# Attention and two MoE layers on one core: later head pairs in key chunks of 128, with the last 64 keys of two pairs packed on four quarters of the array

## The chip, the core and the metric

One core of a Trainium2 chip runs the whole program. The metric is the time on the device in microseconds (us). TensorE (PE) multiplies matrices and writes PSUM, VectorE (DVE), ScalarE (ACT) and GpSimd (POOL) work elementwise, SyncE (SP) issues most DMAs. The kernel before takes 728.23 us, the median of 3 runs (727.34 to 729.0).

## What is computed

Attention over 4 batches, 12 heads, 448 positions, head size 64, then an MLP with a softmax gate and a layer norm, then a mixture of 8 experts. Only the first part is touched:

```python
scores = scale * np.matmul(q, k.transpose(0, 1, 3, 2))
scores = cap * np.tanh(scores / cap)
scores = scores - np.max(scores, axis=-1, keepdims=True)
attn = np.exp(scores)
attn = attn / (np.sum(attn, axis=-1, keepdims=True) + 1e-09)
return np.matmul(attn, v).astype(np.float32)
```

The kernel leaves the row maximum out (the cap bounds the exponent) and divides by the sums at the end.

## The kernel before, in words

Two heads make a pair; pair (b, p) is batch b and heads 2p and 2p+1, and its number is n = 6b + p, 0 to 23. Scores are held transposed, keys on the partitions and 448 queries along the row, so that one tile holds both heads (896 columns). The 448 keys of a pair are cut into four chunks of 112 (`CK`).

A **unit** (`unit`, L949) handles half a pair: `cp` 0 makes the scores of chunks 0 and 1, `cp` 1 those of chunks 2 and 3. Within a unit the order is: scores (`a_scp`, L739), Tanh and Exp on ACT (L765, L770), the product with V (`a_av`, L788), and filler. In a unit with `cp` 1 the V product is that of chunks 0 and 1 of the same pair; in a unit with `cp` 0 it is that of chunks 2 and 3 of the pair before. So V always lags one unit behind the scores.

The first 8 pairs (`PLAIN`) multiply raw float32. From pair 8 on keys and queries are split into a high and a low part of a faster type (kh, kl, qh, ql; `a_split`, L722), and each chunk takes three products, each of two matmuls on the two 64-row halves of the array, one for each head (L758). The V product is plain float32: two matmuls on the two 64-column halves (L800), and in the profile each float32 matmul is two instructions. The sums over keys are first added up on DVE into `es` (`a_esp`, L773: three additions of 896 columns for a pair, L780, L783, L784) and then multiplied with a column of ones on 32-column strips, four at a time, once for two pairs (L812).

**PSUM.** Pool `psA` (L442) has three tiles of two banks under one tag: scores, the MLP's h and y, its transposes lt, and the small tiles sum, rt and rb all take turns in them. Pool `psS` has one bank for the V product (tag B, `btile`, L481) and one for the sums (S). So the V product of a pair cannot start before the copy of the pair before into X has freed the bank (L819, on DVE, or on ACT for some pairs).

**The filler.** From pair 8 on the MLP of the batch before runs in small steps between the attention blocks: `m_h`, `m_act`, `m_tr`, `m_y`, put in by `fill` (L918) at a rate, and by `settle` (L925) when a model of the clock holds that no psA tile is free. `a_fin2` (L855) multiplies a finished batch by its reciprocal sums: three tiles rb_0, rb_1, rb_2, which `finish` (L930) puts into the units of pair p = 1.

**Order.** From pair 8 on only PE's order is written by hand (L1036); ACT, DVE, POOL and SP are ordered ahead of time by a scheduler. Every engine runs its own list strictly in order.

Of the kernel before, what the change touches and what calls it, by code (L numbers as in the profile page):

```python
# [10 lines left out]
F32 = mybir.dt.float32  # L11
F32R = mybir.dt.float32r
F16 = mybir.dt.float16
I32 = mybir.dt.int32
# [8 lines left out]
P = 128  # L23
CK = 112
# [59 lines left out]


@with_exitstack
def attn_moe_kernel(ctx, tc, kq, vv, w_in, w_out, packed, ids, mbias, w1, w2, out):
    nc = tc.nc
    pe, act, dve, pool, sp = nc.tensor, nc.scalar, nc.vector, nc.gpsimd, nc.sync

# [15 lines left out]
    wg_t = pk[:, 1 + NF:]  # L106
    sc8 = con.tile([P, 1], F32, name="sc8")
    epsv = con.tile([P, 1], F32, name="epsv")
    zone = con.tile([CK, 63], F32, name="zone")
    comb = con.tile([P, H], F32, name="comb")  # L110
    sel = con.tile([P, NP, P], F32R, name="sel")
    rh = con.tile([P, S], F32R, name="rh")
# [364 lines left out]
    def atile(nm):  # L477
        clock.take(nm)
        return psA.tile([P, 2, 512], F32, tag="A", name=nm)
# [217 lines left out]
    def direct(b, p):  # L697
        return b * NP + p < DIRECT

    def plain(b, p):  # L700
        return b * NP + p < PLAIN
# [13 lines left out]
            raws[b, p] = [t[:, 0, :], t[:, 1, :]]  # L715

    def v_load(b, p):
        v = ap_.tile([CK, 4, P], F32, tag="v", name=f"v{b}_{p}")
        (act if b * NP + p < VACT else sp).dma_start(out=v, in_=vv[b, p])
        vt[b, p] = v  # L720

    def a_split(b, p, which):  # L722
# [9 lines left out]
    et, est = {}, {}  # L732

    def e_new(nm):
        return ap_.tile([CK, 2, S], F32, tag="e", name=nm, bufs=5)

    exps = {}

    def a_scp(b, p, cp):  # L739

        chunks = (2 * cp, 2 * cp + 1)
        ps = []
        if plain(b, p):
            products = [raws[b, p]]
        else:
            (kh, kl), (qh, ql) = spl[b, p]
            products = [(kh, qh), (kh, ql), (kl, qh)]
        if not plain(b, p):
            settle(2)
        for c in chunks:  # L750
            if not plain(b, p):
                settle()
            t = atile(f"sc{b}_{p}_{c}")
            ps.append(t)
            for i, (k, q) in enumerate(products):
                for j in range(2):
                    r = slice(64 * j, 64 * j + 64)
                    pe.matmul(t[:CK, j, :S], k[r, c * CK:c * CK + CK], q[r], start=(i == 0), stop=(i == len(products) - 1))  # L758
            clock.spend(0.62, "rows")
            clock.work(1.05)  # L760
            clock.leave(f"sc{b}_{p}_{c}", clock.act - clock.t + 0.1)
        clock.work(2.1)
        es = [e_new(f"e{b}_{p}_{c}") for c in chunks]
        for e, t in zip(es, ps):
            act.activation(e, t[:CK, :, :S], AF.Tanh, scale=sc8[:CK])  # L765
        exps[b, p, cp] = es

    def a_exp(b, p, cp):
        for c, e in zip((2 * cp, 2 * cp + 1), exps.pop((b, p, cp))):
            act.activation(e, e, AF.Exp, scale=cap_t[:CK])  # L770
            et[b, p, c] = e

    def a_esp(b, p, cp):  # L773

        if direct(b, p):
            return
        e = [et[b, p, c] for c in (2 * cp, 2 * cp + 1)]
        if cp == 0:
            s = est[b, p] = ap_.tile([CK, 2, S], F32, tag="est", name=f"es{b}_{p}", bufs=2)
            dve.tensor_add(s, e[0], e[1])  # L780
        else:
            s = est[b, p]
            dve.tensor_add(s, s, e[0])  # L783
            dve.tensor_add(s, s, e[1])  # L784

    avt, spt = {}, {}

    def a_av(b, p, chunks=range(4)):  # L788

        if 0 in chunks:  # L790
            avt[b, p] = btile(f"av{b}_{p}")
            if p == 0:
                spt[b] = psS.tile([P, 512], F32, tag="S", name=f"S{b}")
        o, v = avt[b, p], vt[b, p]
        clock.spend(0.75 * len(chunks), "columns")
        if direct(b, p) or p % 2 and 3 in chunks:
            clock.spend(0.75, "strips")
        for c in chunks:
            for j in range(2):
                pe.matmul(o[64 * j:64 * j + 64, :S], v[:, c, 64 * j:64 * j + 64], et[b, p, c][:, j, :],  # L800
                          start=(c == 0), stop=(c == 3))
        if direct(b, p):
            for c in chunks:
                for j in range(2):
                    g = 2 * j + c % 2
                    pe.matmul(spt[b][32 * g:32 * g + 32, :S], zone[:, 31 - p:63 - p], et[b, p, c][:, j, :],  # L806
                              start=(p == 0 and c < 2), stop=(p == NP - 1 and c > 1))
        elif p % 2 and 3 in chunks:
            for j in range(2):
                for i in range(2):  # L810
                    g, pp = 2 * j + i, p - 1 + i
                    pe.matmul(spt[b][32 * g:32 * g + 32, :S], zone[:, 31 - pp:63 - pp], est[b, pp][:, j, :],  # L812
                              start=(p == 1), stop=(p == NP - 1))
        if 3 in chunks:
            x = xtile(b)[:, p, :]
            if convs and b + p:
                later["x"].append(lambda: dve.tensor_copy(x, o[:, :S]))
            else:
                (dve.tensor_copy if b * NP + p in XCD else act.copy)(x, o[:, :S])  # L819
            if p == NP - 1:  # L820
                a_ssb(b)

    sums = {}

    def a_ssb(b):
        ssb = ap_.tile([P, S], F32, tag="es", name=f"ssb{b}", bufs=2)
        act.copy(ssb, spt[b][:, :S])
        sums[b] = ssb
# [120 lines left out]
    def unit(n, cp):  # L949
        nonlocal mp  # L950
        b, p = pairs[n]
        early = plain(b, p) and b > 0
        strips, trs = later["strip"], later["pe"]
        later["strip"], later["pe"] = [], []

        def run(fs):
            while fs:
                fs.pop(0)()

        a_scp(b, p, cp)  # L960
        if n == 1 and not cp:
            a_av(*pairs[0], chunks=(2, 3))
        flush("cast")
        if early and p:
            flush("gate")
            if not cp:
                finish(b - 1, 4)
            else:
                run(strips)
                flush("gate")  # L970
                cv.release()
                mp = tc.alloc_tile_pool(name="mp", bufs=2, reuse_waits="tile")
                do_step()
        a_exp(b, p, cp)
        if early and cp and not p:
            flush("gate", "sub")
            finish(b - 1, 2)
        if cp == 0 and n > 1:
            a_av(*pairs[n - 1], chunks=(2, 3))
        elif cp:  # L980
            a_av(b, p, chunks=(0, 1))
        if convs:
            convs.pop(0)()
        flush("gate", "x")
        run(strips)
        flush("gate")
        if early and p and not cp:
            finish(b - 1, 5)
        run(trs)
        if early and cp and not p:  # L990
            flush("gate")
            finish(b - 1, 3)
        fill(FW[0])
        if b > 0 and not plain(b, p):
            finish(b - 1, 4 * p + 2 * cp)
        flush("sub")
        if n == 1 and cp:
            setup_third(*tables)
        a_esp(b, p, cp)
        if n + 1 < len(pairs):  # L1000
            a_split(*pairs[n + 1], cp)
        fill(FW[1])
        if cp == 1 and n + 2 < len(pairs):
            a_load(*pairs[n + 2])
        if cp == 0 and n + 1 < len(pairs):
            v_load(*pairs[n + 1])
        fill(FW[2])
        if b > 0 and not plain(b, p):
            finish(b - 1, 4 * p + 2 * cp + 1)
        while early and p and sums_:  # L1010
            conv_og(sums_[0], atile(f"po{sums_.pop()}")[:, 0, :NE])
# [24 lines left out]
    with tc.manual_schedule(engines={ET.PE}):  # L1036
        for n in range(FIXED, len(pairs)):
            unit(n, 0)
            unit(n, 1)
        a_av(B - 1, NP - 1, chunks=(2, 3))  # L1040
        for _ in range(ENDS[0]):
            do_step()
        a_sums(B - 1)
        for _ in range(ENDS[1]):
            do_step()
        a_recip(B - 1)
        t = (B - 1) * S // P - 1
# [683 lines left out]
```

## Time and profile before

| | |
|---|---|
| median of 3 runs | 728.23 us |
| the profiled execution: its own time | 729.04 us |
| its span, first to last instruction | 727.2 us |
| TensorE clock granted, of full speed | 0.998 |
| PE / weight loads / DVE / ACT busy | 99% / 76% / 60% / 53% |
| pairs 8 to 23 | about 93 to 366 us of the span |

The span is the core's time line; the profiled execution's own time is 1.84 us longer. A busy share counts the time in which at least one instruction of the engine runs. In the chain of waits, a row gives a start, a length and the work that set the end there; a block such as "sc x12" is a run of 12 matmul instructions.

### The profile page before, as it was taken

The page shows a single profiled execution, that of the slowest core. Times are in us where ns is not written, and L with a number is a line of the kernel's source. Part 1 is how long each engine was busy: PE and PEld are TensorE (multiplying, and loading weights), DVE is VectorE, ACT ScalarE, POOL GpSimd, SP SyncE. Part 2 cuts the span into 40 slices and gives each one's busy share as a digit, 9 for nine tenths or more (in the row PEclk, how much of TensorE's full clock was granted, in tenths as well). Part 3 has the DMA queues.
Part 4 walks back from the last instruction along what each step waited for, and adds up shares of the span by engine and source line. Part 5 has one row for each costly group of instructions (what it writes and reads, how often), then busy time and mean ns, then how long its engine had stood idle before and what let it go on. Part 6 is the DMA issues. An engine that isn't in the chain of part 4 may idle for free.

```text
span 727.2 us, 11226 instructions
## 1 busy us (share of the span) xinstructions
PE 717.3 (99%) x4326; PEld 553.9 (76%) x4326; DVE 432.9 (60%) x727; ACT 384.1 (53%) x518; POOL 109.9 (15%) x196
## 2 busy tenths in 40 slices
PE   8999999999999999999999999999999999999996
PEld 4444566677767777677788999998879998799995
DVE  7999666656755757555366546956255173473632
ACT  6999757765565555556521225344154162553522
POOL 5000102202102012021031211114010220002011
PEclk9999999999999999999999999999999999999999
DMA  7776121211021110110003101578938359584640
GB/s 246 263 271 246 45 83 39 99 39 54 20 86 51 49 61 13 61 36 14 23 22 119 47 33 58 177 279 305 409 107 269 116 182 402 228 251 132 228 158 25
DMA packets 29312, 97.13 MB, mean 134 GB/s; under 512 B 4087, under 2 KB 5125, under 8 KB 28482
## 3 DMA queue, kind: packets, MB, share of 16 engines
q1 hardware_dynamic: 25538, 79.47, 31.4%
q0 software_dynamic: 3568, 16.83, 6.3%
q8 instruction: 36, 0.59, 0.3%
q14 instruction: 26, 0.21, 0.1%
q10 hardware_dynamic: 144, 0.03, 0.0%
HBM read 85.24 MB, written 11.27 MB: 133 GB/s over the span
## 4 chain that ended last, share of the span: by engine, by line
PE 91%; DVE 3%; issue 2%; ACT 1%; DMA 1%; POOL 1%; POOLq 1%; another core or an unknown queue 0%; DVEq 0%; ACTq 0%
PE av L800 10%; PE sc L758 10%; PE h L619 6%; PE h L620 5%; PE h L622 5%; PE y L675 5%; PE y L678 5%; PE y L676 5%; PE poD L1440 3%; PE poD L1442 3%; PE poD L1441 3%; PE phD L1337 3%; PE phD L1339 3%; PE phD L1338 3%; PE S L806 2%
## 5 line engine op out<-in xcount | busy, mean ns | idle before, releaser
L765 ACT ACTIVATE e<-sc,sc 112x896 f32<-112x896 f32 x96 | 94.5, 1003 | 50.7 <-PE sc L758 50.6
L770 ACT ACTIVATE e<-e,pk 112x896 f32<-112x896 f32 x96 | 98.0, 1044 | 1.7
L800 PE MATMUL av<-e,v 112*64 112x448 f32 x384 | 82.8, 552 | 0.0
L675 PE MATMUL y<-wouh,lh 128*128 128x392 f32 (+1 forms) x224 | 77.7, 347 | 0.0
L676 PE MATMUL y<-woul,lh 128*128 128x392 f32 (+1 forms) x224 | 75.8, 339 | 0.0
L678 PE MATMUL y<-wouh,ll 128*128 128x392 f32 (+1 forms) x224 | 71.5, 339 | 0.3 <-DVE ll L665 0.3
L619 PE MATMUL h<-winh,xh 128*128 128x512 f32 x168 | 69.0, 410 | 0.0
L620 PE MATMUL h<-winl,xh 128*128 128x512 f32 x168 | 65.8, 392 | 0.0
L622 PE MATMUL h<-winh,xl 128*128 128x512 f32 x168 | 61.2, 391 | 0.0
L800 PEld LDWEIGHTS av<-e,v 112*64 112x64 f32 x384 | 23.3, 136 | 41.6 <-issue 29.5
L675 PEld LDWEIGHTS y<-wouh,lh 128*128 128x128 f32 x224 | 42.0, 188 | 8.4 <-issue 7.1
L1281 DVE TENSOR_TENSOR wl_D<-raw_D,wh_D 128x768 fp32r<-128x768 f32 (+1 forms) x28 | 29.9, 1071 | 27.9 <-ACT wh_D L1280 27.8
L619 PEld LDWEIGHTS h<-winh,xh 128*128 128x128 f32 x168 | 31.5, 188 | 16.6 <-issue 9.3
L1440 PE MATMUL poD<-wh_D,hhD 128*128 128x384 f32 x128 | 43.0, 336 | 0.0
L1441 PE MATMUL poD<-wl_D,hhD 128*128 128x384 f32 x128 | 42.8, 334 | 0.0
L1442 PE MATMUL poD<-wh_D,hlD 128*128 128x384 f32 x128 | 42.8, 334 | 0.0
L676 PEld LDWEIGHTS y<-woul,lh 128*128 128x128 f32 x224 | 42.1, 188 | 0.6
L1281 DVE TENSOR_TENSOR wl_H<-raw_H,wh_H 128x768 fp32r<-128x768 f32 (+1 forms) x28 | 29.2, 1069 | 22.1 <-ACT wh_H L1280 21.3
L678 PEld LDWEIGHTS y<-wouh,ll 128*128 128x128 f32 x224 | 41.9, 188 | 0.6 <-DVE ll L665 0.6
L1280 ACT CAST wh_D<-raw_D 128x768 fp32r<-128x768 f32 (+1 forms) x28 | 26.0, 933 | 30.6 <-DMA raw_D<-in_w_dram 30.3
L729 POOL TENSOR_TENSOR kl<-kqr,kh 128x448 fp32r<-128x448 f32 x16 | 18.5, 1153 | 125.5 <-ACT kh L728 69.0
L1338 PE MATMUL phD<-xl_D,wh_D 128*128 128x512 f32 x96 | 37.4, 389 | 0.0
(396 smaller groups left out, 1578.7 us busy)
## 6 DMA issues: line engine op xcount, KB each, us to landing
kqr<-in_kq_dram SPq DMA_DIRECT2D x20, 448.0 KB, 3.1
rawc<-in_w_out_dram SPq DMA_DIRECT2D x8, 768.0 KB, 5.2
rawc<-in_w_in_dram SPq DMA_DIRECT2D x6, 1024.0 KB, 4.8
raw_D<-in_w_dram SPq DMA_DIRECT2D x12, 512.0 KB, 5.1
wr_T<-in_w_dram SPq DMA_DIRECT2D x16, 384.0 KB, 6.0
raw_D<-in_w_dram SPq DMA_DIRECT2D x16, 384.0 KB, 4.6
wr_T<-in_w_dram SPq DMA_DIRECT2D x12, 512.0 KB, 10.1
raw_H<-in_w_dram SPq DMA_DIRECT2D x12, 512.0 KB, 7.4
```

The lines of the kernel that those rows point to most:

```text
L619: pe.matmul(o, s["xh"][d], winh[d][:, c], start=(d == 0), stop=False)
L620: pe.matmul(o, s["xh"][d], winl[d][:, c], start=False, stop=False)
L622: pe.matmul(o, s["xl"][i], winh[i][:, c], start=False, stop=(i == ND - 1))
L675: pe.matmul(o, s["lh"][f], wouh[f][:, c], start=(f == 0), stop=False)
L676: pe.matmul(o, s["lh"][f], woul[f][:, c], start=False, stop=False)
L678: pe.matmul(o, s["ll"][i], wouh[i][:, c], start=False, stop=(i == NF - 1))
L758: pe.matmul(t[:CK, j, :S], k[r, c * CK:c * CK + CK], q[r], start=(i == 0), stop=(i == len(products) - 1))
L765: act.activation(e, t[:CK, :, :S], AF.Tanh, scale=sc8[:CK])
L770: act.activation(e, e, AF.Exp, scale=cap_t[:CK])
L800: pe.matmul(o[64 * j:64 * j + 64, :S], v[:, c, 64 * j:64 * j + 64], et[b, p, c][:, j, :], start=(c == 0), stop=(c == 3))
L1440: pe.matmul(p, hh[:, f, o], wh[:, c], start=(f == 0), stop=False)
L1441: pe.matmul(p, hh[:, f, o], wl[:, c], start=False, stop=False)
```

## The change

Pairs 8 to 23 cut their keys into three chunks of 128 and a rest of 64. The rests of an even pair and the odd pair after it share one score tile, called h: partitions 0 to 63 hold the even pair's last 64 keys, 64 to 127 the odd pair's. Its four matmuls (two pairs, two heads) are raw float32, each on one 64x64 quarter of the array. Chunks: the even pair has (0, 1) and (2, h), the odd pair (0, 1) and (2).

The V product of h goes to a psA tile of its own, q (`a_quarters`), in the unit of the odd pair with `cp` 0: four matmuls on four quarters. It is copied into X for both pairs (DVE, 128x896), and the V product of the other chunks is then added to X (`tensor_add` on DVE) where it was copied before (11 times on DVE, 5 on ACT). The half of h that belongs to a pair is added to `es` by a DVE addition of 64 partitions, so that each pair still has three additions. V is loaded in another layout: 128x4x128 for an even pair, 128x3x128 for an odd one.

```diff
+    def chunks_of(b, p, cp):
+        if plain(b, p):
+            return (2 * cp, 2 * cp + 1)
+        return (((0, 1), (2, "h")), ((0, 1), (2,)))[p % 2][cp]
@@ a_scp
         if not plain(b, p):
-            settle(2)
+            settle(len(chunks))
         for c in chunks:
             if not plain(b, p):
                 settle()
             t = atile(f"sc{b}_{p}_{c}")
             ps.append(t)
-            for i, (k, q) in enumerate(products):
-                for j in range(2):
-                    r = slice(64 * j, 64 * j + 64)
-                    pe.matmul(t[:CK, j, :S], k[r, c * CK:c * CK + CK], q[r], start=(i == 0), stop=(i == len(products) - 1))
+            if c == "h":
+                for g in range(2):
+                    k, q = raws[b, p + g]
+                    for j in range(2):
+                        r = slice(64 * j, 64 * j + 64)
+                        pe.matmul(t[64 * g:64 * g + 64, j, :S], k[r, 3 * P:S], q[r], start=True, stop=True)
+            else:
+                for i, (k, q) in enumerate(products):
+                    for j in range(2):
+                        r = slice(64 * j, 64 * j + 64)
+                        pe.matmul(t[:m, j, :S], k[r, c * m:c * m + m], q[r], start=(i == 0), stop=(i == len(products) - 1))
@@ a_esp
-            dve.tensor_add(s, s, e[0])
-            dve.tensor_add(s, s, e[1])
+            dve.tensor_add(s, s, e[2])
+        if cp != p % 2:
+            r = slice(64 * (p % 2), 64 * (p % 2) + 64)
+            h = et[b, p - p % 2, "h"]
+            dve.tensor_add(s[r], s[r], h[r])
@@ a_av
             if convs and b + p:
                 later["x"].append(lambda: dve.tensor_copy(x, o[:, :S]))
+            elif plain(b, p):
+                (dve.tensor_copy if b * NP + p in XCD else act.copy)(x, o[:, :S])
             else:
-                (dve.tensor_copy if b * NP + p in XCD else act.copy)(x, o[:, :S])
+                dve.tensor_add(x, x, o[:, :S])
+    def a_quarters(b, p):
+        settle()
+        t = atile(f"q{b}_{p}")
+        for g in range(2):
+            r = slice(64 * g, 64 * g + 64)
+            for j in range(2):
+                c = slice(64 * j, 64 * j + 64)
+                pe.matmul(t[c, g, :S], vt[b, p][r, 3, c], et[b, p, "h"][r, j, :], start=True, stop=True)
+        clock.spend(0.75, "quarters")
+        dve.tensor_copy(xtile(b)[:, p:p + 2, :], t[:, :, :S])
@@ unit
         if cp == 0 and n > 1:
-            a_av(*pairs[n - 1], chunks=(2, 3))
+            m = pairs[n - 1]
+            if not plain(*m) and not m[1] % 2:
+                a_quarters(*m)
+            a_av(*m, chunks=(2, 3) if plain(*m) else (2,))
         elif cp:
             a_av(b, p, chunks=(0, 1))
```

How the lists of instructions move is shown at three places. In the names below the first figure is the head pair p within its batch, and a last long figure is only the tile's number; sc are scores, av the V product, q the quarters, X the pair's output, es the summed exponentials, rb the reciprocal sums.

PE, batch 1, the units of pair p = 3 (n = 9). Before:

```order
L758 MATMUL sc_3_1_1054<-qh_3_991,kl_3_953 112x448 x2
L800 MATMUL av_2_981<-e_2_2_975,v_2_836 64x448 x2
L800 MATMUL av_2_981<-e_2_3_976,v_2_836 64x448 x2
L758 MATMUL sc_3_2_1080<-qh_3_991,kh_3_952 112x448 x2
L758 MATMUL sc_3_2_1080<-ql_3_992,kh_3_952 112x448 x2
L758 MATMUL sc_3_2_1080<-qh_3_991,kl_3_953 112x448 x2
L758 MATMUL sc_3_3_1087<-qh_3_991,kh_3_952 112x448 x2
L758 MATMUL sc_3_3_1087<-ql_3_992,kh_3_952 112x448 x2
L758 MATMUL sc_3_3_1087<-qh_3_991,kl_3_953 112x448 x2
L800 MATMUL av_3_1100<-e_3_0_1061,v_3_956 64x448 x2
```

and now:

```order
L782 MATMUL sc_3_1_1052<-qh_3_989,kl_3_953 128x448 x2
L619 MATMUL h_1023<-winh_116,xh_0_1015 128x512
L620 MATMUL h_1023<-winl_122,xh_0_1015 128x512
L622 MATMUL h_1023<-winh_116,xl_0_1016 128x512
L861 MATMUL q_2_1068<-e_2_h,v_2_836 64x448 x4
L829 MATMUL av_2_979<-e_2_2_973,v_2_836 64x448 x2
L782 MATMUL sc_3_2_1086<-qh_3_989,kh_3_952 128x448 x2
L782 MATMUL sc_3_2_1086<-ql_3_990,kh_3_952 128x448 x2
L782 MATMUL sc_3_2_1086<-qh_3_989,kl_3_953 128x448 x2
L829 MATMUL av_3_1096<-e_3_0_1059,v_3_956 64x448 x2
```

One score chunk and one V chunk are gone, a block q stands between, and three filler matmuls come ahead of it.

DVE, batch 2, the unit of pair p = 1 (n = 13) with `cp` 0, from the end of the MLP's normalization (L640) on. Before:

```order
L640 TENSOR_SCALAR u_1494<-u_1494,sm_1495 128x1024
L819 COPY X_1573<-av_0_1468 128x448
L865 TENSOR_TENSOR X_806<-X_806,rb_0_1575 128x896
L780 TENSOR_TENSOR es_1_1579<-e_1_0_1563,e_1_1_1564 112x896
L865 TENSOR_TENSOR X_806<-X_806,rb_1_1587 128x896
L865 TENSOR_TENSOR X_806<-X_806,rb_2_1606 128x896
```

and now:

```order
L640 TENSOR_SCALAR u_1472<-u_1472,sm_1473 128x1024
L863 COPY X_1555<-q_0_1550 128x896
L805 TENSOR_TENSOR es_1_1564<-e_1_0_1541,e_1_1_1542 128x896
L850 TENSOR_TENSOR X_1555<-X_1555,av_0_1446 128x448
L907 TENSOR_TENSOR X_806<-X_806,rb_0_1560 128x896
L812 TENSOR_TENSOR es_1_1564<-es_1_1564,e_0_h 64x896
L907 TENSOR_TENSOR X_806<-X_806,rb_1_1579 128x896
L680 SCALAR_TENSOR_TENSOR lg<-y_1489,sm_1136,bias_t 128x8
L907 TENSOR_TENSOR X_806<-X_806,rb_2_1594 128x896
```

The product with rb_0 was second behind the normalization and is now fourth, behind the first es addition; the one with rb_1 has a further es addition ahead of it.

PE, batch 3, the unit of pair p = 1 (n = 19) with `cp` 0, at rb_1. Before:

```order
L678 MATMUL y_2534<-wouh_128,ll_2447 128x392
L858 MATMUL rb_1_2545<-rh,sel 128x448 x2
L675 MATMUL y_2534<-wouh_131,lh_2446 128x392
L676 MATMUL y_2534<-woul_139,lh_2446 128x392
L678 MATMUL y_2534<-wouh_129,ll_2447 128x392
```

and now:

```order
L678 MATMUL y_2487<-wouh_128,ll_2395 128x392
L900 MATMUL rb_1_2498<-rh,sel 128x448 x2
L900 MATMUL rb_2_2503<-rh,sel 128x448 x2
L675 MATMUL y_2487<-wouh_131,lh_2394 128x392
L676 MATMUL y_2487<-woul_139,lh_2394 128x392
```

Before, 17 matmuls of y stood between rb_1 and rb_2; now none does, and they follow rb_2.

## Rows read from the trace of the kernel before

**Rows 1.** The page, busy time and share of the span of each engine
```profile
PE 717.3 (99%) x4326; PEld 553.9 (76%) x4326; DVE 432.9 (60%) x727; ACT 384.1 (53%) x518; POOL 109.9 (15%) x196
```

**Rows 2.** Stretches: busy us of PE, PEld, DVE, ACT, POOL; clock; DMA share, GB/s
```profile
93.00:184.00 91.00, 90.58 (x519) 60.48 (x518) 59.04 (x88) 61.43 (x79) 14.21 (x24) 1.00 0.17 55
...
275.00:366.00 91.00, 91.00 (x510) 65.08 (x512) 51.93 (x80) 54.58 (x71) 12.38 (x24) 1.00 0.09 29
```

**Rows 3.** All waits of PE from 93 to 366 us (us, times, longest)
```profile
PE sc L758 <- DVE sm L642: 0.2, 1, 0.2
PE rb L858 <- ACT e L765: 0.2, 1, 0.2
```

**Rows 4.** The chain of waits: start us, length us, what
```profile
256.12 0.89 PE S L812 x8
...
307.02 0.24 PE h L622
307.26 0.18 PE y L675
...
312.07 1.41 PE sc L758 x12
313.48 1.65 PE av L800 x8
```

**Rows 5.** PE in order of time around 253 us: start us, length us
```profile
252.72 0.34 PE L678 MATMUL y<-wouh,ll 128*128 128x384 f32 x1
252.99 0.46 PE L758 MATMUL sc<-qh,kh 64*112 64x448 f32 x2
253.28 0.37 PE L758 MATMUL sc<-ql,kh 64*112 64x448 f32 x2
253.49 0.36 PE L758 MATMUL sc<-qh,kl 64*112 64x448 f32 x2
...
256.05 0.58 PE L812 MATMUL S<-es,zone 112*32 112x448 f32 x4
...
256.94 0.45 PE L675 MATMUL y<-wouh,lh 128*128 128x384 f32 x1
257.23 0.33 PE L676 MATMUL y<-woul,lh 128*128 128x384 f32 x1
```

**Rows 6.** Groups by line, 93 to 366 us: busy us, mean ns, idle before
```profile
L800 PEld LDWEIGHTS av<-e,v 112*64 112x64 f32 x264 | 16.0, 136 | 26.0 <-issue 24.5 <-ACT e L770 0.6 <-DVE es L780 0.3
L819 DVE COPY X<-av 128x448 f32<-128x448 f32 x12 | 7.5, 624 | 21.8 <-PE av L800 21.8
L865 DVE TENSOR_TENSOR X<-X,rb 128x896 f32<-128x896 f32 x6 | 6.5, 1084 | 0.6 <-PE rb L858 0.6
L812 PEld LDWEIGHTS S<-es,zone 112*32 112x32 f32 x64 | 1.3, 108 | 5.6 <-issue 5.6
```

**Rows 7.** ACT in order of time: a unit's first and last step; u's Exp
```profile
281.06 1.12 ACT L634 ACTIVATE u<-h,sm 128x1024 f32<-128x1024 f32 x1 [2.38 <-DVE sm L633]
282.37 0.51 ACT L602 CAST xh<-X 128x384 fp32r<-128x384 f32 x1
...
312.90 1.01 ACT L765 ACTIVATE e<-sc,sc 112x896 f32<-112x896 f32 x1 [2.34 <-PE sc L758]
...
315.91 1.04 ACT L770 ACTIVATE e<-e,pk 112x896 f32<-112x896 f32 x1
```

**Rows 8.** DVE in order of time: u's chain with rb_2; a first es
```profile
282.29 1.22 DVE L635 TENSOR_TENSOR u<-u,h 128x1024 f32<-128x1024 f32 x1
...
284.00 1.28 DVE L638 BATCH_NORM_STATS2 bn<-u 128x6 f32<-128x512 f32 x2
285.20 1.07 DVE L865 TENSOR_TENSOR X<-X,rb 128x896 f32<-128x896 f32 x1
...
286.73 0.75 DVE L640 TENSOR_SCALAR u<-u,sm 128x1024 f32<-128x1024 f32 x1
...
316.99 1.09 DVE L780 TENSOR_TENSOR es<-e,e 112x896 f32<-112x896 f32 x1 [1.19 <-ACT e L770]
```

More of the change, by code (lines that the diff above doesn't have):

```diff
@@ L86, in attn_moe_kernel @@
 @with_exitstack
-def attn_moe_kernel(ctx, tc, kq, vv, w_in, w_out, packed, ids, mbias, w1, w2, out):
+def attn_moe_kernel(ctx, tc, kq, vv, vl, w_in, w_out, packed, ids, mbias, w1, w2, out):
     nc = tc.nc
@@ L108, in attn_moe_kernel @@
     epsv = con.tile([P, 1], F32, name="epsv")
-    zone = con.tile([CK, 63], F32, name="zone")
+    zone = con.tile([P, 63], F32, name="zone")
     comb = con.tile([P, H], F32, name="comb")
@@ L717, in v_load @@
     def v_load(b, p):
-        v = ap_.tile([CK, 4, P], F32, tag="v", name=f"v{b}_{p}")
-        (act if b * NP + p < VACT else sp).dma_start(out=v, in_=vv[b, p])
+        n = b * NP + p
+        v = ap_.tile([P, 4, P], F32, tag="v", name=f"v{b}_{p}")
+        if plain(b, p):
+            v = v[:CK]
+            sp.dma_start(out=v, in_=vv[n])
+        elif n % 2:
+            sp.dma_start(out=v[:, 0:3, :], in_=vl[(n - PLAIN) // 2, :, 4:7, :])
+        else:
+            sp.dma_start(out=v, in_=vl[(n - PLAIN) // 2, :, 0:4, :])
         vt[b, p] = v
@@ L734, in e_new, with keys_of @@
     def e_new(nm):
-        return ap_.tile([CK, 2, S], F32, tag="e", name=nm, bufs=5)
+        return ap_.tile([P, 2, S], F32, tag="e", name=nm, bufs=5)
     exps = {}
+    def chunks_of(b, p, cp):
+        if plain(b, p):
+            return (2 * cp, 2 * cp + 1)
+        return (((0, 1), (2, "h")), ((0, 1), (2,)))[p % 2][cp]
+    def keys_of(b, p):
+        return CK if plain(b, p) else P
     def a_scp(b, p, cp):
-        chunks = (2 * cp, 2 * cp + 1)
+        chunks = chunks_of(b, p, cp)
+        m = keys_of(b, p)
         ps = []
@@ L754, in a_scp @@
             ps.append(t)
-            for i, (k, q) in enumerate(products):
-                for j in range(2):
-                    r = slice(64 * j, 64 * j + 64)
-                    pe.matmul(t[:CK, j, :S], k[r, c * CK:c * CK + CK], q[r], start=(i == 0), stop=(i == len(products) - 1))
-            clock.spend(0.62, "rows")
+            if c == "h":
[4 more added lines that the diff above has]
+                        pe.matmul(t[64 * g:64 * g + 64, j, :S], k[r, 3 * P:S], q[r], start=True, stop=True)
+            else:
+                for i, (k, q) in enumerate(products):
+                    for j in range(2):
+                        r = slice(64 * j, 64 * j + 64)
+                        pe.matmul(t[:m, j, :S], k[r, c * m:c * m + m], q[r], start=(i == 0), stop=(i == len(products) - 1))
+            clock.spend(*((0.75, "quarters") if c == "h" else (0.62, "rows")))
             clock.work(1.05)
             clock.leave(f"sc{b}_{p}_{c}", clock.act - clock.t + 0.1)
-        clock.work(2.1)
-        es = [e_new(f"e{b}_{p}_{c}") for c in chunks]
+        clock.work(1.05 * len(chunks))
+        es = [e_new(f"e{b}_{p}_{c}")[:m] for c in chunks]
         for e, t in zip(es, ps):
-            act.activation(e, t[:CK, :, :S], AF.Tanh, scale=sc8[:CK])
+            act.activation(e, t[:m, :, :S], AF.Tanh, scale=sc8[:m])
         exps[b, p, cp] = es
     def a_exp(b, p, cp):
-        for c, e in zip((2 * cp, 2 * cp + 1), exps.pop((b, p, cp))):
-            act.activation(e, e, AF.Exp, scale=cap_t[:CK])
+        m = keys_of(b, p)
+        for c, e in zip(chunks_of(b, p, cp), exps.pop((b, p, cp))):
+            act.activation(e, e, AF.Exp, scale=cap_t[:m])
             et[b, p, c] = e
@@ L776, in a_esp @@
             return
-        e = [et[b, p, c] for c in (2 * cp, 2 * cp + 1)]
+        e = [et[b, p, c] for c in range(2 + cp)]
         if cp == 0:
-            s = est[b, p] = ap_.tile([CK, 2, S], F32, tag="est", name=f"es{b}_{p}", bufs=2)
+            s = est[b, p] = ap_.tile([P, 2, S], F32, tag="est", name=f"es{b}_{p}", bufs=2)
             dve.tensor_add(s, e[0], e[1])
@@ L794, in a_av @@
         o, v = avt[b, p], vt[b, p]
+        end = 3 if plain(b, p) else 2
         clock.spend(0.75 * len(chunks), "columns")
-        if direct(b, p) or p % 2 and 3 in chunks:
+        if direct(b, p) or p % 2 and end in chunks:
             clock.spend(0.75, "strips")
@@ L800, in a_av @@
                 pe.matmul(o[64 * j:64 * j + 64, :S], v[:, c, 64 * j:64 * j + 64], et[b, p, c][:, j, :],
-                          start=(c == 0), stop=(c == 3))
+                          start=(c == 0), stop=(c == end))
         if direct(b, p):
@@ L805, in a_av @@
                     g = 2 * j + c % 2
-                    pe.matmul(spt[b][32 * g:32 * g + 32, :S], zone[:, 31 - p:63 - p], et[b, p, c][:, j, :],
+                    pe.matmul(spt[b][32 * g:32 * g + 32, :S], zone[:CK, 31 - p:63 - p], et[b, p, c][:, j, :],
                               start=(p == 0 and c < 2), stop=(p == NP - 1 and c > 1))
-        elif p % 2 and 3 in chunks:
+        elif p % 2 and end in chunks:
             for j in range(2):
@@ L813, in a_av @@
                               start=(p == 1), stop=(p == NP - 1))
-        if 3 in chunks:
+        if end in chunks:
             x = xtile(b)[:, p, :]
@@ L1039, in attn_moe_kernel @@
             unit(n, 1)
-        a_av(B - 1, NP - 1, chunks=(2, 3))
+        a_av(B - 1, NP - 1, chunks=(2,))
         for _ in range(ENDS[0]):
@@ L1708 @@
     ]
+    pv = inputs["v"].reshape(B * NP, 2, S, D)
+    lv = pv[PLAIN:].reshape(-1, 2, 2, S, D)
+    full = lv[:, :, :, :3 * P].reshape(-1, 2, 2, 3, P, D).transpose(0, 1, 4, 3, 2, 5).reshape(-1, 2, P, 3, P)
+    half = lv[:, :, :, 3 * P:].transpose(0, 1, 3, 2, 4).reshape(-1, P, 1, P)
     host = {
         "kq": c(_np.stack([headsT(inputs["k"]), headsT(inputs["q"])], axis=3)),
-        "vv": c(inputs["v"].reshape(B, NP, 2, 4, CK, D).transpose(0, 1, 4, 3, 2, 5).reshape(B, NP, CK, 4, P)),
+        "vv": c(pv[:PLAIN].reshape(PLAIN, 2, 4, CK, D).transpose(0, 3, 2, 1, 4).reshape(PLAIN, CK, 4, P)),
+        "vl": c(_np.concatenate([full[:, 0], half, full[:, 1]], axis=2)),
         "w_in": c(inputs["moe_w_in"]).view(_np.int64),
@@ L1724 @@
         args.append(nc.dram_tensor(f"in_{name}_dram", a.shape, _mybir.dt.from_np(a.dtype), kind="ExternalInput").ap())
-    args[5] = args[5].bitcast(I32).rearrange("p (t w) -> p t w", w=2)
+    args[6] = args[6].bitcast(I32).rearrange("p (t w) -> p t w", w=2)
     args.append(nc.dram_tensor("out_0_dram", (NT + 1, DM), F32, kind="ExternalOutput").ap())
```

## The prediction

> **What bounds the kernel now.** The page comes first: PE is busy 99% of the span, the next engine 76 and 60% [rows 1]. An average can hide stages, so I cut the span: the change only touches pairs 8 to 23, 93 to 366 us, and there PE is busy in every third, DVE for 52 to 59 us of 91 and ACT for 55 to 61 [rows 2]. The list of PE's waits in that stretch holds two of 0.2 us [rows 3]. So each us that leaves PE's list leaves the time, as long as nobody makes PE wait; what must be looked for is a new wait, and it will come from DVE or ACT.
>
> **What PE loses and gains.** The chain of waits gives blocks with all that lies around them [rows 4]: two score chunks 1.41, two V chunks 1.65, the sums S 0.89. Within a block [rows 5] the score matmuls come in pairs 0.21 apart (253.28 to 253.49), so six take 1.22 and 0.19 is fixed; one chunk then costs 3 x 0.2035 + 0.19 = 0.80. The S block has eight instructions, of which four start together: two rounds. A single V chunk has four instructions, two at a time: also two rounds, so 0.89, and 0.03 more since a weight load of 64 columns takes 136 ns and one of 32 takes 108 [rows 6]: 0.92.
> - Scores: 16 of the 32 score blocks shrink from two chunks to one: 16 x (1.41 - 0.80) = -9.8.
> - V product: 16 of 32 blocks from 1.65 to 0.92: -11.7.
> - Quarter blocks: 8 of scores (h) and 8 of V (q), each four matmuls in two instructions. No row shows row halves and column halves at once. The rows show two row halves side by side (sc), and four column strips side by side (S). Four at once gives two rounds, 0.92; two at once gives four rounds, as the V block of two chunks, 1.65. I take 0.92, nearest to the S rows, which run four different moving tiles at a time: +14.7, bound above by +26.4.
> - Seven of the eight q blocks have filler between the scores and themselves, so PE leaves the tiled order and returns. Into a block the last full matmul takes 0.27 for 0.18 (252.72 to 252.99), out of it the first takes 0.29: +0.09 +0.11, seven times: +1.5.
> - 128 key columns for 112 cost nothing: y loads 128 columns for each of its matmuls, and those follow at 0.18 for 392 columns [rows 4], the same rate as here.
>
> Sum on PE: -9.8 - 11.7 + 14.7 + 1.5 = **-5.3 us**.
>
> The Trainium skill (TensorE: Matmul & The Clock Gate, Part 3 on packing) says that row and column tiles compose, with a few ns for each further tile; no run here shows it. By it the quarter block is 0.92 too.
>
> **ACT and DMA.** ACT loses 16 x (Tanh + Exp, about 2.0) and five copies; it had 30 us of 91 free, so that is worth nothing by itself. V moves the same bytes in as many loads. The raw keys and queries are held one unit longer, which the next load but one waits for; its data is needed a unit (some 8 us) later still. DVE gains 8 copies of 128x896 (priced as the addition of that size, 1.08 [rows 6]) and five additions of 128x448 (as the copy, 0.62): 12 us in 273, which its free third would cover.
>
> **Where DVE does not cover it.** What matters is its place in the list. The bank of the V product is freed by the addition into X, and that now stands behind the copy of q and mostly behind the first `es` addition as well, which must wait for the odd pair's second Exp. Let 0 be the start of a unit's first Tanh. Its score block ends at 0.58 (313.48 against 312.90), the four ACT steps end at 4.05, and DVE's `es` starts at 4.09 [rows 7, 8]. On DVE an operation starts 0.08 ahead of the end of the last (284.00 + 1.28 against 285.20 [rows 8]). I walked PE's, ACT's and DVE's lists through all eight odd pairs; in four PE comes first.
> 1. Pair n = 9 (first place shown in the order). PE: 0.58, three h 0.81, q 0.09 + 0.92, V 0.92, one score chunk 0.80: it is at the next V product at 4.1. DVE: `es` 4.09, X addition 5.10 to 5.72. **Wait 1.6.**
> 2. Pair n = 11. There is hardly any filler, and ACT is eight steps behind: the second Exp ends after 12 steps, 12.1. DVE has `es`, the copy of q, the half addition of h and then X: 12.1 + 1.01 + 1.00 + 1.01 + 0.62 = 15.7. PE, from the Tanh of pair 10: V and S 2.4, chunk and h 4.1, V 5.8, six y 7.0, scores 8.5, nine y 10.2, q and V 12.1, six y 13.3, chunk 14.2. **Wait 1.5.**
> 3. Pair n = 13 (second place shown). Each rb tile takes the psA tile of the one before. DVE: `es` 4.09, X 5.10, rb_0 5.64, half of h 6.64, rb_1 7.65 to 8.73. The next score chunk takes rb_1's tile, and PE is there at 7.3 (0.58, y 1.24, q 2.25, V 3.2, rb_0, 15 y, rb_1, rb_2). **Wait 1.4.**
> 4. Pair n = 19 (third place shown). The MLP's h ends just ahead of the unit, so ACT does u's Exp between the two Tanh, and q and rb_0 wait for their tiles, 0.35 and 0.4. DVE begins u's product 1.23 after that Exp began (282.29 against 281.06), at 2.27. Before, 3.98 us later the product with an rb was done (285.20 + 1.07); now the copy of q, the X addition and the rest of u's chain come in ahead, 1.00 + 0.54 + 0.67 + 0.12: 8.6. PE is at rb_2 at 6.0. **Wait 2.6, and 3.4 in all.**
>
> The other odd pairs (15, 17, 21, 23) have 15 or more filler matmuls ahead of the tile in question: PE arrives at 6.8 or later, DVE is done at 5.7.
>
> The Trainium skill (TensorEngine Tiling, Performance Considerations) warns that tiling speeds up the array and not the emptying of PSUM. By the busy shares [rows 2] that would not bite and the sum would stay at -5.3; by the four walks it does, for 7.9 us.
>
> **Forecast.** -5.3 + 1.6 + 1.5 + 1.4 + 3.4 = +2.6 us. From the profiled execution's own 729.04 that is 731.6; it lies 0.8 above the median of the runs shown, 728.23, so the median comes to **730.8 us**. With an error of 1 us for PE's sum and of 0.4 for each wait, its own range is 728.5 to 733.5. A change within 0.2% (1.5 us) cannot be told from none.
>
> **Rivals.**
> - The waits do not arise (faster). Place: the V product's one bank, and rb's tiles. What decides is whether DVE's last addition ends ahead of PE's arrival; if the four places together cost under 3.8 us, the kernel is faster by over 0.2%. For it: before, the same three tiles and one bank cost PE 0.4 us [rows 3], and the planner had room. Against: the copy into X then stood first in DVE's list, or on ACT. With none of the waits 722.9, with half 726.9. Chance 0.25.
> - Part of them: one of the four large waits is hidden, 728 to 729.5, no change. Chance 0.12.
> - The quarters do not run four at once, so the change does not do what it says. 16 x 0.73 = +11.7 on PE; as PE then arrives later, each of the four waits shrinks by 0.7: 730.8 + 11.7 - 2.9 = 739.6. For it: no row shows a quarter. Against: the S rows. Chance 0.10.
> - The forecast, 0.53, of which 0.08 lies within 0.2%.
>
> So: faster 0.22 (the first rival, less its part near no change), same 0.23 (0.03 of the first, 0.12, 0.08), slower 0.55 (0.45 and 0.10). The range has to reach the first rival and leaves out the quarters at two a time: 723 to 736.
>
> **What will show it.** Right: q and h blocks near 0.9 in the chain; single score and V blocks 0.8 and 0.9; in PE's waits DVE's X (the addition) before av, and X (the products with rb) before rb and sc, some 7 to 9 us together; the same PE list else. PE's clock stays at 1.00. Wrong: quarter blocks of 1.6; or PE's waits in the stretch under 4 us, which would make it faster; or PE waiting for the key and query loads, which I hold to be early.

## The result, and the profile after

The changed kernel takes 733.7 us, the median of 7 runs (731.27 to 736.85), the kernel before 727.4 (7 runs, 726.9 to 729.0): ratio 1.0085, interval 1.0068 to 1.0102. It is slower, as the likeliest case had it, and within the range of 723 to 736; but the loss is 5 to 7 us where 2.6 was forecast.

The profiled execution took 734.7 us, its span is 733.0. The page of the changed kernel, busy time and share of the span:

```profile
PE 712.8 (97%) x4294; PEld 546.6 (75%) x4294; DVE 443.8 (61%) x740; ACT 365.5 (50%) x497; POOL 110.4 (15%) x196
```

PE is busy 4.5 us less than before [rows 1] and yet the span is 5.8 longer: the rest must be idle time. The stretches of pairs 8 to 23 show where (columns as in [rows 2]):

```profile
93.00:184.00 91.00, 84.33 (x479) 52.78 (x476) 60.80 (x89) 53.83 (x69) 15.13 (x24) 0.98 0.16 55
...
275.00:366.00 91.00, 88.12 (x490) 62.20 (x489) 53.50 (x82) 46.68 (x62) 12.59 (x23) 0.98 0.10 34
```

PE fell from 90.6 and 91.0 of 91 us to 84.3 and 88.1. DVE, whose busy time grew by 1.8 and 1.6 us, is still idle for a third or more. The granted clock is 0.98 where it was 1.00. All waits of PE from 93 to 372 us (us, times, longest), to be set against [rows 3]:

```profile
PE av L829 <- DVE X L850: 3.5, 2, 1.8
PE rb L900 <- DVE X L907: 2.3, 1, 2.3
PE sc L782 <- DVE X L907: 1.6, 1, 1.6
PE h L619 <- DVE xh L602: 1.1, 1, 1.1
PE q L861 <- ACT e L789: 0.5, 1, 0.5
PE sc L782 <- DVE sm L643: 0.5, 1, 0.5
PE sc L782 <- ACT ys L689: 0.2, 1, 0.2
```

That is 9.7 us where there were 0.4. The first three rows and the q row are the four places of the prediction. Place 1 (pair 9) in order of time, first on PE, then on DVE (start us, length us, what, and the idle time ahead of it):

```profile
110.89 0.98 PE L861 MATMUL q<-e_h,v 64*64 64x448 f32 x8
111.80 0.97 PE L829 MATMUL av<-e,v 128*64 128x448 f32 x4
112.70 0.47 PE L782 MATMUL sc<-qh,kh 64*128 64x448 f32 x2
...
115.25 1.72 PE L829 MATMUL av<-e,v 128*64 128x448 f32 x8 [1.68 <-DVE X L850]
```

```profile
111.93 1.09 DVE L863 COPY X<-q 128x896 f32<-128x896 f32 x1 [1.82 <-PE q L861]
113.57 1.09 DVE L805 TENSOR_TENSOR es<-e,e 128x896 f32<-128x896 f32 x1 [0.55 <-ACT e L795]
114.58 0.61 DVE L850 TENSOR_TENSOR X<-X,av 128x448 f32<-128x448 f32 x1
```

The q block starts at 110.89 and the next block at 111.80: 0.91, and 0.90 for the V product of one chunk. DVE has nothing to do at 113.02, with the V product finished, but its list holds `es` first, which waits 0.55 for the second Exp; the addition that frees the bank ends at 115.19 and PE goes on at 115.25.

Place 3 (pair 13), DVE and then PE, and the granted clock behind it (the last three figures of a window's row are the clock, the DMA share and GB/s):

```profile
174.98 1.09 DVE L812 TENSOR_TENSOR es<-es,e_h 64x896 f32<-64x896 f32 x1
176.10 1.09 DVE L907 TENSOR_TENSOR X<-X,rb 128x896 f32<-128x896 f32 x1
```

```profile
177.25 0.47 PE L782 MATMUL sc<-qh,kh 64*128 64x448 f32 x2 [1.56 <-DVE X L907]
...
178.05 2.93 PE L829 MATMUL av<-e,v 128*64 128x448 f32 x8
```

```profile
177.00:178.00 1.00, 0.75 (x6) 0.48 (x6) 1.00 (x3) 0.78 (x2) 0.00 (x0) 1.00 0.00 0
178.00:179.00 1.00, 1.00 (x6) 0.44 (x6) 1.00 (x5) 1.00 (x5) 0.00 (x0) 0.71 0.00 0
179.00:180.00 1.00, 1.00 (x4) 0.24 (x2) 0.23 (x1) 1.00 (x3) 0.90 (x1) 0.50 0.02 8
```

The score block waits for the product with rb_1, which stands behind half of h. And then something that was not forecast: after the pause, 1.2 us after PE has started again, the clock falls to 0.50, the lower of its two levels (1.2 GHz), and a V block that takes 1.66 elsewhere takes 2.86 (178.05 to 180.91). It is back at 1.00 by 182. The same follows the wait at place 4, from 287.7 to 291.1:

```profile
287.68 1.08 PE L900 MATMUL rb<-rh,sel 128*128 128x448 f32 x2 [2.29 <-DVE X L907]
```

After places 1 and 2 of this execution the clock stayed at 1.00.

So the excess comes from waits and from PE at the lower clock. In the profiled execution the two can be added up. Its two stretches at 0.50 (178.4 to 181.8 and 287.7 to 291.1) cost about half their length, 1.7 us each, by my estimate; the forecast's -5.3 for PE, 9.3 more of waits and these 3.4 make +7.4, and it took 7.3 us longer than the kernel before. How much of the second there is differs from run to run, as the mean clock of the seven shows: 0.999 at 731.27 and 731.9; 0.997 at 733.22; 0.995 at 733.7; 0.994 at 734.7; 0.992 at 736.42 and 736.85. Without such a stretch the kernel stands at 731 to 732, some 4 to 4.5 us above the kernel before, where 2.6 was forecast.

### The profile page after: what moved, and what is told of

Same layout as the page of the kernel before. It is cut to its first block, busy times and chain, and to the rows that moved or that the text cites. A ratio compares the mean times of both kernels' runs of the same rounds, so it can differ in the third digit from the quotient of the medians.

```text
span 733.0 us, 11175 instructions
## 1 busy us (share of the span) xinstructions
PE 712.8 (97%) x4294; PEld 546.6 (75%) x4294; DVE 443.8 (61%) x740; ACT 365.5 (50%) x497; POOL 110.4 (15%) x196
## 5 line engine op out<-in xcount | busy, mean ns | idle before, releaser
L789 ACT ACTIVATE e<-sc,sc 128x896 f32<-128x896 f32 (+1 forms) x80 | 78.5, 1003 | 62.2 <-PE sc L782 62.2
L795 ACT ACTIVATE e<-e,pk 128x896 f32<-128x896 f32 (+1 forms) x80 | 81.4, 1044 | 1.1
L829 PE MATMUL av<-e,v 128*64 128x448 f32 (+1 forms) x320 | 72.1, 563 | 4.2 <-DVE X L850 3.5
L829 PEld LDWEIGHTS av<-e,v 128*64 128x64 f32 (+1 forms) x320 | 18.8, 137 | 44.8 <-issue 26.3
L665 DVE TENSOR_TENSOR ll<-lt,lh 128x512 fp32r<-128x512 f32 x28 | 19.3, 689 | 33.1 <-ACT lh L664 32.9
```

The source lines that it names most:

```text
L789: act.activation(e, t[:m, :, :S], AF.Tanh, scale=sc8[:m])
L795: act.activation(e, e, AF.Exp, scale=cap_t[:m])
```

## The experiments

Theory A is the prediction's: PE waits because DVE's additions stand late in its list, and, new, the clock falls after such waits. Theory B: the quarter blocks cost more than the trace shows, or the bank is not what PE waits for. Every run has the kernel before beside it on the same chip.

**1. The addition into X ahead of `es`** (x_first). One edge on DVE's list for each odd pair; PE's, POOL's and SP's lists are as they were.

```diff
+xadd[b, p] = dve.tensor_add(x, x, o[:, :S]).ins      # in a_av
-dve.tensor_add(s, e[0], e[1])                        # in a_esp
+with tc.issue_after(xadd[b, p - 1]) if p % 2 else nullcontext():
+    dve.tensor_add(s, e[0], e[1])
```

> One edge alone: on DVE the addition of the V product into X now stands ahead of the odd pair's first es addition; PE's, POOL's and SP's lists stay as they are. Theory A (PE waits because DVE's additions stand late in its list, and the clock falls after such waits): PE's waits before av fall from 3.5 us to under 0.6, the one before sc at place 3 (1.6) to under 0.6, since rb_1's product moves up as well; place 4 (2.3) stays. Time 728 to 730.5. Theory B (the bank is not what PE waits for, or the quarter blocks themselves cost more than the trace shows): the waits turn up before another block and the time stays at 733 to 735.

Measured: 726.35 us (11 runs), ratio 0.9988 (0.9979 to 0.9997). This edge is worth 7 us, more than expected. Of PE's waits three rows say why; DVE at place 1 follows:

```profile
PE rb L900 <- DVE X L907: 2.3, 1, 2.3
PE h L619 <- DVE xh L602: 1.1, 1, 1.1
...
PE av L829 <- DVE X L850: 0.2, 1, 0.2
```

```profile
111.85 1.09 DVE L863 COPY X<-q 128x896 f32<-128x896 f32 x1 [1.81 <-PE q L861]
113.05 0.62 DVE L850 TENSOR_TENSOR X<-X,av 128x448 f32<-128x448 f32 x1
113.59 1.08 DVE L805 TENSOR_TENSOR es<-e,e 128x896 f32<-128x896 f32 x1
```

The addition now fits into the gap in which DVE had waited for Exp, and `es` starts at 113.59 where it started at 113.57: it lost nothing. The waits before av fell from 3.5 to 0.2 and the one at place 3 is gone: 4.9 of the 7.3 us. The rest fits the clock that is no longer lost: the profiled run's mean is 0.999, although the wait at place 4 is as long as it was. There the block behind the wait takes 0.65, where it took 1.08 in the changed kernel:

```profile
280.91 0.65 PE L900 MATMUL rb<-rh,sel 128*128 128x448 f32 x2 [2.29 <-DVE X L907]
```

**2. The rb tiles one unit later** (fin_later), and **3. both edits** (both).

```diff
-FIN = ((2, 3, 4, 4, 5), (2, 3, 4, 5, 5))
+FIN = ((2, 3, 4, 4, 5), (2, 3, 6, 6, 7))
```

> The three rb tiles are put one unit later (into the unit with cp 1, which has no q tile); the av places stay. Theory A: PE's waits before rb (2.3) and before sc behind rb_1 (1.6) go, those before av (3.5) stay. Time 728.5 to 731. Theory B: 733 to 735.

> Both edits together. Theory A: about 7.4 of the 9.7 us of PE's waits go, with them the clock's loss (mean granted clock 0.998 or more, runs within 2 us of each other): the kernel before, 727.4, less some 6.9 that PE saves, plus some 2.3 of waits left = 722.8, within 721.5 to 725. Theory B: 730 or more, and the clock's mean stays near 0.995.

Measured: 732.32 (5 runs), ratio 1.0064 (1.005 to 1.0077) for the rb tiles alone, above the range that Theory A gave. The waits at places 3 and 4 went, save 0.3, but the row "PE av <- DVE X" grew from 3.5 in two waits to 5.6 in four. In place 3's unit PE now stands one block later, before the V product, for the addition into X that still stands behind `es`; and behind place 2's wait, but not behind this equally long one, the clock falls to 0.50, from 143.4 to 146.9:

```profile
143.40 3.25 PE L829 MATMUL av<-e,v 128*64 128x448 f32 x8 [1.84 <-DVE X L850]
...
176.60 1.72 PE L829 MATMUL av<-e,v 128*64 128x448 f32 x8 [1.84 <-DVE X L850]
```

Both edits: 723.07 (5 runs, within 0.45 us of each other, clock 0.998 and 0.999), ratio 0.9943 (0.993 to 0.9957), faster than the kernel before. All waits of PE that are left:

```profile
PE h L619 <- DVE xh L602: 1.1, 1, 1.1
PE av L829 <- DVE X L850: 0.5, 2, 0.2
PE sc L782 <- DVE sm L643: 0.3, 1, 0.3
```

With the same quarter blocks and few of the waits the kernel is close to where the first rival's arithmetic had put it (722.9). Theory B falls.

**4. Waits in the kernel before** (waits_in_before), to see whether the clock belongs to the pauses or to the new blocks.

```diff
-(dve.tensor_copy if b * NP + p in XCD else act.copy)(x, o[:, :S])
+for _ in range(6 if b * NP + p in (8, 12, 16, 20) else 1):
+    (dve.tensor_copy if b * NP + p in XCD else act.copy)(x, o[:, :S])
```

(Pair 8 is added to `XCD`.)

> The kernel before, with nothing of the change: the V product of pairs 8, 12, 16 and 20 is copied into X six times on DVE instead of once (pair 8 on DVE instead of ACT), so that its one bank comes free late and PE has to wait there, 1 to 3 us at each. Theory A (the clock falls after waits of PE, whatever the blocks): time is 727.4 plus the sum of PE's waits in the trace (4 to 10 us) plus some 1.7 us for each stretch at the lower clock, of which there are one or more; the mean clock of the runs is 0.992 to 0.997. Theory B (the lower clock belongs to the quarter blocks or to the new order): the time is 727.4 plus PE's waits alone, and the clock stays at 0.998 or more in every run.

Measured: 735.61 (4 runs, clock 0.994 in each), ratio 1.0112 (1.0097 to 1.0128). Only at pair 9 did the copies make PE wait, for 3.9 us; another 1.0 arose before h. PE there, and the granted clock:

```profile
116.27 3.25 PE L800 MATMUL av<-e,v 112*64 112x448 f32 x8 [3.88 <-issue]
119.46 1.97 PE L655 MATMUL lt<-ident,u 128*128 128x128 f32 x8
```

```profile
114.00:115.00 1.00, 0.00 (x0) 0.00 (x0) 0.93 (x3) 1.00 (x2) 1.00 (x1) 1.00 0.00 0
115.00:116.00 1.00, 0.00 (x0) 0.00 (x0) 0.97 (x2) 1.00 (x2) 0.09 (x1) 0.56 0.00 0
...
118.00:119.00 1.00, 1.00 (x5) 0.06 (x2) 0.77 (x1) 0.00 (x0) 0.00 (x0) 0.50 0.23 43
```

Without a quarter block in the program the clock falls while PE stands, and the V block behind it takes 3.19 for 1.65 [rows 4], the transposes 1.62 for the 0.85 that they take in x_first. PE's waits, 5.3 us against 0.4, account for 4.9 of the 8.2 us that were added; what is left, 3.3, is about what PE's blocks lose at the lower clock (my estimate: PE works at 0.50 from 116.27 to about 121.9, which costs 2.8). The loss comes with the pause and needs no quarter block.

**5. A shorter pause** (waits_short): three copies instead of six.

> As waits_in_before, with three copies instead of six: PE's wait before av at pair 9 shrinks from 3.9 to some 1.8 us, about as long as the waits of the changed kernel. Theory A (it is the length of PE's pause that decides whether the clock falls): in waits_in_before all four runs had a clock of 0.994; here some runs or all stay at 0.998 or more, at 729 to 730, and those with a lower clock lie some 1.7 us higher. Theory D (any wait of PE costs the clock): every run is at 0.996 or less, 731 to 732.

Measured: 730.75 (6 runs), ratio 1.0031 (1.0019 to 1.0044). The wait in the profile is 1.9 us, and the clock behind it stays:

```profile
115.11 1.72 PE L800 MATMUL av<-e,v 112*64 112x448 f32 x8 [1.90 <-issue]
```

```profile
116.00:117.00 1.00, 1.00 (x8) 0.30 (x5) 0.43 (x1) 1.00 (x2) 0.00 (x0) 1.00 0.00 0
```

The runs: 0.999 at 731.2, 729.07 and 729.62; 0.997 at 731.16 and 730.84; 0.995 at 730.67. Theory D (any wait costs the clock) falls. Theory A does not stand either. The runs of lower clock are not 1.7 us longer, as it had it, and of the 2.9 us that were added PE's waits give 1.9; for the other 1.0 I have no row. And length alone does not decide: the two waits of 1.84 in run 2 and the two of 2.29 (the changed kernel and run 1) went one each way. Runs of the kernel before show 0.997 to 0.999 with no relation to their times. The mean also holds the end of the span, where PE has nothing left to do and the clock is at 0.50 too, from 724 us on in the kernel before and from 725.6 on in run 6. A difference of 0.002 in the mean therefore says nothing; the 0.992 to 0.995 of the changed kernel do. What decides whether a pause of this length costs the clock stays open.

**6. q's copy on ACT** (q_act): is it the place in the list, or DVE's load?

```diff
-dve.tensor_copy(xtile(b)[:, p:p + 2, :], t[:, :, :S])
+act.copy(xtile(b)[:, p:p + 2, :], t[:, :, :S])
```

> The changed kernel with q's copy into X on ACT instead of DVE, nothing else; the additions into X still stand behind es. Theory A (the place in DVE's list is the cause): the es addition waits for the second Exp in any case, so PE's wait before av at place 1 (1.7) and the one before sc at place 3 (1.6) stay as they are within 0.3; place 2 (1.8) and place 4 (2.3) lose up to one copy, 1.0, each. PE's waits 7.5 to 9.5, time 730.5 to 733. Theory C (DVE has too much work, wherever it stands): 8 x 1.09 = 8.7 of the 12 us that the change adds on DVE go, and with them two thirds of the waits: PE's waits under 4, time under 728.

Measured: 732.43 (5 runs), ratio 1.007 (1.0056 to 1.0084). DVE is busy 8.2 us less (435.6 for 443.8 on the pages), and PE waits nearly as long (8.5 us in all):

```profile
PE av L829 <- DVE X L850: 2.5, 2, 1.7
PE rb L900 <- DVE X L907: 1.9, 1, 1.9
PE sc L782 <- DVE X L907: 1.6, 1, 1.6
```

Places 1 and 3 did not move, place 2 lost 1.0 and place 4 0.4. Moving one addition ahead of another gave 7.3 us; taking 8.2 of the 10.9 us that the change adds to DVE's busy time off the engine gave 1.3. Theory C falls.

**7. No q tile** (h_in_av): the V product of h is added up in the bank of its pair, on two quarters at a time.

```diff
-a_quarters(*m)                                       # in unit
+pe.matmul(o[64 * j:64 * j + 64, :S], w[r, 3, 64 * j:64 * j + 64],
+          et[b, p - p % 2, "h"][r, j, :], start=False, stop=False)
...
-dve.tensor_add(x, x, o[:, :S])
+(dve.tensor_copy if b * NP + p in XCD else act.copy)(x, o[:, :S])
```

> No q block and no q tile: the last 64 keys' V product of a pair is two matmuls of 64 rows and 64 columns, added up in the same bank as its chunks (the even pair's in front of its chunk 2, the odd pair's in front of its chunk 1); X is copied as in the kernel before; rb one unit later as in fin_later. Counting on PE against the kernel with both edits (723.07): 16 V blocks grow from 0.9 to 1.65 (+11.7), 8 q blocks of 0.91 and 7 ways out of the tiled order at 0.2 go (-8.7): +3.0, so 726.0, and with the 0.5 of waits before av gone 725 to 727; the quarters packed four at a time are then worth 3 us. Rival: with only two quarters of one half of the rows at a time each such matmul costs as much as four at once do, which is what the sum has, but adding to a bank that full-height matmuls also write makes it wait for them: 728 or more. Other rival: without 8 copies on DVE the kernel is as fast as with both edits, 723.5 or less.

Measured: 731.61 (5 runs), ratio 1.0053 (1.0039 to 1.0067), with 1.7 us of waits: 8.5 above both edits where 3.0 was expected. PE at the V product of pair 8:

```profile
111.50 0.97 PE L831 MATMUL av<-e_h,v 64*64 64x448 f32 x4
112.40 0.97 PE L833 MATMUL av<-e,v 128*64 128x448 f32 x4
113.30 0.47 PE L782 MATMUL sc<-qh,kh 64*128 64x448 f32 x2
```

Four instructions on two quarters take 0.90 (111.50 to 112.40), eight on four took 0.91: the quarters do run four at once, and half of them saves nothing. My sum had 1.65 for two V steps in a row, but that holds only for two of the same shape; here each pays 0.90. An even pair then pays 0.90 more, an odd one 3 x 0.90 for 1.66, so 1.04 more: 8 x 1.94 = 15.5, less the 8.7 for q, is 6.8 of the 8.5; for 1.7 I have no row. The first rival (a bank that full-height matmuls also write makes them wait) shows in no row: two such blocks in one bank follow each other after 0.90, as two in different banks did. The Trainium skill (TensorEngine Tiling (Array Packing), Key Properties) says that a change of the tiling mode drains TensorE; the 0.90 for each of these blocks, against 0.83 for each half of a pair of equal ones, is consistent with that.

**8. The halves of h on POOL** (half_pool_both), on top of both edits.

```diff
-dve.tensor_add(s[r], s[r], h[r])
+pool.tensor_add(s[r], s[r], h[r])
```

> The kernel with both edits, and the additions of a half of h to es (64 x 896, 16 of them, 18.1 us) on POOL instead of DVE. Theory A: what is left of PE's waits stands behind DVE (h behind xh 1.1, av 0.5, sc 0.3); xh moves up by the half addition and the row's reduction, so the 1.1 goes and the time falls by 1 to 723.07 - 1.1 = 722.0, within 721.3 to 722.8. Rival: POOL takes 1.33 for 128 x 448 (kl), so by its length some 2.7 for a half of h; if es then comes late for the sums, PE waits before S, and the time is 724 or more.

Measured: 726.67 (12 runs), ratio 0.9991 (0.9982 to 0.9999): 3.6 slower than with DVE. The 1.1 before h did go, but three waits of 1.2 arose before sc. Neither theory had the reason. POOL, DVE and PE of this kernel around one of them:

```profile
192.22 2.10 POOL L812 TENSOR_TENSOR es<-es,e_h 64x896 f32<-64x896 f32 x1 [14.90 <-ACT e_h L795]
194.72 1.35 POOL L736 TENSOR_TENSOR kl<-kqr,kh 128x448 fp32r<-128x448 f32 x1 [0.39 <-DVE kh L735]
```

```profile
192.90 1.68 DVE L735 CAST kh<-kqr 128x448 fp32r<-128x448 f32 x1
...
194.97 1.35 DVE L735 CAST qh<-kqr 128x448 fp32r<-128x448 f32 x1
```

```profile
198.25 0.47 PE L782 MATMUL sc<-qh,kh 64*128 64x448 f32 x2 [1.15 <-DVE sm L642]
```

and DVE of the kernel with both edits, the same cast:

```profile
193.34 0.38 DVE L735 CAST kh<-kqr 128x448 fp32r<-128x448 f32 x1
```

A cast of 0.38 us takes 1.68 and 1.35 beside an operation of POOL, and ends about 0.25 us after that one (194.58 against 194.32, 196.32 against 196.07). The Trainium skill (SBUF — State Buffer, Who interferes with whom) says that DVE and GpSimd share a pair of SBUF ports under an exclusive lock; these rows agree. The row's chain on DVE comes late, and with it the psA tile that the score block needs. The other two waits look alike: ahead of the one at 312.3 the casts take 1.69 and 1.35, ahead of the one at 176.0 a subtraction (ql) takes 2.51 where it takes 0.63 alone, each beside an operation of POOL.

**9. xh ahead of the half of h** (xh_first), on top of both edits: one edge more, at pair 8.

```diff
+c = (act.copy if t in XHA else dve.tensor_copy)(xh[:, :, off:off + n], src).ins   # in m_split; row 1's is kept
+with tc.issue_after(st["c"]):                                                     # in a_esp, pair 9, cp 0
+    dve.tensor_add(est[1, 2][:64], est[1, 2][:64], et[1, 2, "h"][:64])
```

> The kernel with both edits, and one more edge on DVE: at pair 8 the cast xh of the next row goes ahead of the addition of the half of h, which moves behind it; PE's list stays. Theory A: PE's wait before h for xh (1.1) goes, and nothing else moves: 723.07 - 1.1 = 722.0, within 721.4 to 722.6. Rival: the wait turns up at the next block (h behind xl or u's chain), 722.7 to 723.4.

Measured: 721.78 (5 runs), ratio 0.9911 (0.9899 to 0.9924): the fastest, 6 us ahead of the kernel before and within Theory A's range. All waits of PE:

```profile
PE av L832 <- DVE X L853: 0.5, 2, 0.2
PE sc L783 <- DVE sm L644: 0.3, 1, 0.3
PE sc L783 <- ACT ys L690: 0.2, 1, 0.2
```

## Why the prediction was right, and where it was off

- **PE's sum (-5.3): right.** The blocks are 0.91 (q and h), 0.90 (one V chunk) and 0.80 (one score chunk, 177.25 to 178.05), where 0.92, 0.92 and 0.80 were counted; two V chunks take 1.66. With these the sum is -9.8 - 12.2 + 14.6 + 1.4 = -6.0 (seven times 0.20 is 1.4 and not 1.5). Checked by time: x_first is 1.0 us under the kernel before with 4.4 us more of waits, so PE's list gave 5.4; both edits 4.3 + 1.5 = 5.8; xh_first 6.1 + 0.6 = 6.7, a little beyond the 1 us of error that was allowed.
- **Quarters four at once: right**, by the 0.91 for eight instructions and the 0.90 for four (run 7). That agrees with what the Trainium skill says (TensorE: Matmul & The Clock Gate, Part 3), that row and column tiles compose. The rival with two at a time falls. The Trainium skill's warning (TensorEngine Tiling (Array Packing), Performance Considerations) that tiling does not speed up the emptying of PSUM fits only in part. PE does wait for the bank at places 1 and 2, but with the same operations in another order these waits fall from 3.5 to 0.2 (run 1): it was the order and not the rate.
- **The four waits: right in place and cause, and in the sum with some luck.** Forecast 1.6, 1.5, 1.4 and 3.4, in all 7.9; measured 1.7, 1.8, 1.6 and 2.8 (2.3 before rb and 0.5 before q), in all 7.9. The equal sums are luck: place 2 was 0.3 longer and place 4 0.6 shorter, since rb_0 did not wait. Runs 1 to 3 show that they are what the change loses: take them away and it gains. Run 6 shows that it is the place in DVE's list and not its load.
- **The first rival (the waits do not arise) is what two edits of the order make of it**: 723.07 measured for its 722.9. That they agree to 0.2 is luck: 722.9 was counted from 728.23, and this run's kernel before took 727.38 and 1.5 us of the waits were left.
- **"Some 7 to 9 us together" holds for the rows that it names** (DVE's X before av, rb and sc: 7.4), but all of PE's new waits together are 9.3, where the forecast had 7.9. The eight walks went through the odd pairs only. The 1.1 before h lies in pair 8, an even one, where the half of h and a row's reduction stand ahead of xh on DVE (run 9 takes it away); 0.5 behind sm and 0.2 behind ys are new too.
- **"PE's clock stays at 1.00" is the step that failed.** I took the clock from a trace in which PE never stood for more than 0.2 us [rows 3] and priced a wait at its own length. The runs with a mean of 0.999 lie at 731.3 and 731.9, as -5.3 + 9.3 = +4.0 would have it; the median, at 0.995, lies 2 us above, and the profiled execution lost some 3.4 us to its two stretches at 0.50. Run 4 shows the same loss behind a pause with none of the change in the program.
- **ACT's relief was overstated**: 16 times Tanh and Exp and five copies would be over 32 us, and the pages show 18.6 (384.1 to 365.5), since the eight tiles h need Tanh and Exp too. No term of the sum hangs on it.

## What to carry to other kernels

When an instruction gets a second job, ask where it stands in its engine's list and what the one ahead of it waits for: here an addition of 0.6 us behind one that waited for ACT cost more than the whole change saved, and one edge gave it back at no cost to the other. Price a new wait of PE as its length and, for a part of the runs, the blocks behind it at half the clock (here some 1.7 us more for such a wait). Work moved to POOL to relieve DVE was not free on DVE here.

## What was not expected of the hardware

- The granted clock falls to its lower level, 0.50, after a pause of PE of 1.56 us (place 3, 1.2 us after PE works again), after pauses of 1.84 (run 2) and 2.29 us (place 4) as PE works again, and during one of 3.9 us (run 4). It did not after pauses of 1.68 and 1.83 in the same execution as the first, nor after a second one of 1.84 in run 2, 1.9 in run 5 and 2.29 at the same place in run 1. PE's blocks then take up to twice as long: 2.86 and 3.19 for 1.66 and 1.65.
- A cast on DVE of 0.38 us takes 1.35 and 1.68 beside POOL's operations of 1.35 and 2.10 (run 8).
- POOL adds 64 x 896 in 2.1 us, less than the 2.7 that I had estimated from its 1.33 for 128 x 448.
